# Three transposes of attention outputs moved from TensorE to DMA in a fused attention and mixture-of-experts kernel

## The chip, the cores and the metric

The kernel runs on one core of one Trainium2 chip. The core has a matrix engine (TensorE, PE in the profile), a vector engine (VectorE, DVE), an activation engine (ScalarE, ACT), a general engine (GpSimd, POOL) and a sequencer that mostly issues transfers (SyncE, SP). Each runs its own list of instructions in order, and waits on semaphores for the others. Sixteen DMA engines move data.

The metric is the device time of one execution in microseconds (us). The kernel before was run six times: the median is 678.63 us, the runs lie between 677.74 and 682.57.

## The reference

Two stages. First, attention over 4 batches, 8 heads, 768 positions and 64 dimensions a head. Each query sees its near keys (fewer than 16 positions away) and one summary key per block of 32 (the maximum of the block's keys, with the mean of its values):

```python
k_sum = k.reshape(B, H, nb, block, D).max(axis=3)
v_sum = v.reshape(B, H, nb, block, D).mean(axis=3)
scores_l_m = np.where(mask_l, scale * np.matmul(q, k.transpose(0, 1, 3, 2)), -1e9)
scores_s = scale * np.einsum('bhsd,bhnd->bhsn', q, k_sum) + np.log(block)
a = softmax(np.concatenate([scores_l_m, scores_s], axis=-1))
attn = np.matmul(a, np.concatenate([v, v_sum], axis=2))
```

Its output, as 3072 tokens of 512 features (`x`), goes to eight experts with a routing matrix that is normalised by rows and columns in turn, eight times:

```python
P = np.exp(x @ w_gate - max)
for _ in range(8):
    P /= P.sum(1, keepdims=True) + 1e-09
    P /= P.sum(0, keepdims=True) + 1e-09
    P *= N / E
for e in range(E):
    out += P[:, e:e + 1] * (np.maximum(x @ w1[e], 0.0) @ w2[e])
```

## The kernel before

**Tiling.** Attention is worked on in 16 pairs of heads; pair `i` belongs to batch `i // 4`, so pairs 12 to 15 are the last batch. Pairs 0 to 3 are done in halves, the others whole (`pair_whole`, line 687). A pair passes through these steps, named as the planner names them: the keys and queries are transposed (`tr`, line 295, tile tkq) and copied out (kT, qT); block sums of values (vs); block maxima of keys (km); scores (sg) and their exponential (er); the mask (em) and the edges of the window (Ee); scores of the block summaries (ss) and their exponential; `values` (line 389, tile av), the product with the values; `normalize` (line 487), which divides by the sums and writes the result as fp16 to the tile xs, 128 tokens by 6 x 128 features; `to_xT` (line 502), six 128x128 transposes on TensorE into a PSUM bank (tx); `x_out` (line 509), the copy from there to the persistent tile xT, on ScalarE or VectorE.

xs has two buffers for whole pairs, so `normalize` of pair i waits until the transposes of pair i-2 have read theirs (`U["xt", i - 2]`, line 712).

**Row copies.** `near_values` (line 346) copies edge rows of the values into the tile Ve by four small DMAs from SyncE. It waits until the values of pair i-2 have read that buffer. Until the output stores near the end of the program, SyncE issues nothing else.

**Fillers.** Attention alone does not fill TensorE, so the first expert (expert 0: `hidden_mm`, tile hps, and `project_mm`, tile yps, lines 198 to 211) is worked in between, for half batches whose xT is complete. When a batch's four pairs are through, `logits` (line 515, tile lp) computes its routing logits from xT, for all four pairs. After those of the last batch comes the routing normalisation (lines 1070 to 1101), beside the rest of expert 0 and the first groups of expert 1.

**The order.** It is made by a planner at build time (`Plan`, line 34). Each step is a unit with an engine, a planned cost in us, the units that it depends on, a priority, PSUM buffers that it opens or uses, and a lag, the time from its end until its result may be used. The planner simulates the engines with these figures and emits the units in the order in which they would start; the order in each engine's list is what it leaves behind. A cost that changes can move work on all engines. After attention the order is written out by hand (from line 1149): 6.08 us a group in the trace, experts 1 to 7 in a scheme that uses seven products in place of eight.

Of the kernel before, what the change touches and what calls it, by code (L numbers as in the profile page):

```python
# [33 lines left out]
class Plan:  # L34
# [12 lines left out]
    def add(self, eng, cost, fn, deps=(), prio=0.0, opens=(), uses=(), lag=0.0):  # L47
        u = Unit(eng, cost, fn, [d for d in deps if d is not None], prio, list(opens), lag)
        for b in list(opens) + list(uses):
            b.users.append(u)  # L50
        if uses and eng != "PE":
            u.prio -= 100.0
        self.waiting.append(u)
        return u
# [62 lines left out]
def kernel(  # L117
# [10 lines left out]
    nc = tc.nc  # L128

    B, H, S, D = q.shape  # L130
    G = S // 128
# [7 lines left out]
    PB = H // 2  # L139
# [20 lines left out]
    xT = persist.tile([128, KD, N], FP16)  # L160
# [34 lines left out]
    def copy(eng, out, in_):  # L195
        (nc.scalar.copy if eng == "ACT" else nc.vector.tensor_copy)(out=out, in_=in_)
# [19 lines left out]
    NE = 2  # L216
# [9 lines left out]
    if True:  # L226
# [16 lines left out]
        add = plan.add  # L243

        at, units = {}, {}

        def bank(tag, name, dtype=FP32):
            pool, n = (mps, 3) if tag == "m" else (aps, NA)
            return pool.tile([128, 2048 // mybir.dt.size(dtype)], dtype, tag=tag, name=name, bufs=n)
# [45 lines left out]
        def tr(i, z, tag):  # L295
            st = at.pop(("st", i, z))
            t = at["t", i, z] = bank(tag, "tkq", BF16)
            for g in range(G):
                if i < PB:
                    for j in range(2):  # L300
                        nc.tensor.transpose(t[64 * j:64 * j + 64, g * 128:(g + 1) * 128],
                                            st[:, j, g, :], ident)
                else:
                    nc.tensor.transpose(t[:, g * 128:(g + 1) * 128],  # L304
                                        st[:, g, :, :].rearrange("p j d -> p (j d)"), ident)

        def tr_out(eng, i, z):
            r, src = i % NB, at.pop(("t", i, z))[:, 0:S]
            dst = (kT[r][:], qT[r][:, W:W + S])[z]
            if i < PB:  # L310
                dst = dst.rearrange("c (p g) -> c p g", g=G)
                src = src.rearrange("c (g p) -> c p g", g=G)
            copy(eng, dst, src)
# [32 lines left out]
        def near_values(i):  # L346

            sv, ve = v_x[i % NQ], V_e[i % NE]
            for j in range(2):
                c0, q0 = VD * j, 64 + 32 * j  # L350
                nc.sync.dma_start(out=ve[q0 + W:q0 + 2 * W, 1:G, c0:c0 + VD],
                                  in_=sv[128 - W:128, j, 0:G - 1, :])
                nc.sync.dma_start(out=ve[q0:q0 + W, 0:G - 1, c0:c0 + VD],
                                  in_=sv[0:W, j, 1:G, :])

        def scores(i, h):
            sg = at["sg", i, h] = banks2("sg")
            for s in range(HG):
                for j in range(2):
                    score_mm(i, sg[:, j, s * LIVE:(s + 1) * LIVE], j, HG * h + s, 0, LIVE)  # L360

        def score_exp(i, h):
            if h == 0:
                at["er", i] = attn.tile([128, 2, G, LIVE], BF16, tag="er", name="er", bufs=2)
                at["em", i] = attn.tile([128, 2, G, 128], BF16, tag="em", name="em", bufs=2)
            nc.scalar.activation(
                out=at["er", i][:, :, HG * h:HG * (h + 1), :].rearrange("p j g l -> p j (g l)"),
                in_=at.pop(("sg", i, h))[:, :, 0:HG * LIVE], func=AF.Exp, bias=0.0, scale=SCALE)

        def masks(i, h):  # L370
            c = slice(HG * h, HG * (h + 1))
            nc.vector.tensor_tensor(
                out=at["em", i][:, :, c, :], in0=at["er", i][:, :, c, W:W + 128],
                in1=band[:, None, None, W:W + 128].to_broadcast([128, 2, HG, 128]), op=ALU.mult)

        def edges(i):
            ee, er = E_e[i % NE], at.pop(("er", i))
            for j in range(2):
                q0 = 64 + 32 * j
                nc.vector.tensor_tensor(out=ee[q0:q0 + 32, 0:G - 1, 128 - W:128],  # L380
                                        in0=er[0:32, j, 1:G, 0:W],
                                        in1=band[0:32, None, 0:W].to_broadcast([32, G - 1, W]),
                                        op=ALU.mult)
                nc.vector.tensor_tensor(out=ee[q0:q0 + 32, 1:G, 0:W],
                                        in0=er[96:128, j, 0:G - 1, W + 128:LIVE],
                                        in1=band[96:128, None, W + 128:LIVE].to_broadcast([32, G - 1, W]),
                                        op=ALU.mult)
# [114 lines left out]
        def to_xT(i, h=None):  # L502
            t = at.pop(("xs", i, h or 0))
            tx = at["tx", i, h] = bank("a", "tx", FP16)
            for g in range(G if h is None else HG):
                nc.tensor.transpose(tx[:, g * 128:(g + 1) * 128],  # L506
                                    t[:, g, :, :].rearrange("p j d -> p (j d)"), ident16)

        def x_out(eng, i, h=None):
            n, t0 = (S, 0) if h is None else (HS, h * HS)  # L510
            t0 += i // PB * S
            copy(eng, xT[:, i % PB, t0:t0 + n], at.pop(("tx", i, h))[:, 0:n])
# [92 lines left out]
        U = {}  # L605
# [79 lines left out]
            return U.get((what, n % PB, n // PB)) if n >= 0 else None  # L685

        def pair_whole(i, prio):
            U["near", i] = add("SP", 0.4, lambda: near_values(i), [U["v", i], U.get(("A", i - NE, 1))], prio,
                               lag=3.5)
            for h in range(2):  # L690
                buf = Buffer("s")
                U["S", i, h] = add("PE", 0.28, lambda h=h: scores(i, h),
                                   [U["kT", i, 0], U["kT", i, 1], U.get(("ed", i - 2))], prio, opens=[buf])
                U["X", i, h] = add("ACT", 0.97, lambda h=h: score_exp(i, h), [U["S", i, h]], prio, uses=[buf])
                U["mk", i, h] = add("DVE", 0.56, lambda h=h: masks(i, h),
                                    [U["X", i, h], U.get(("A", i - 2, 1))], prio)
            U["ed", i] = add("DVE", 0.78, lambda: edges(i),
                             [U["X", i, 0], U["X", i, 1], U["mk", i, 1], U.get(("A", i - NE, 1))], prio)
            bufs = [Buffer("a"), Buffer("a")]
            U["ss", i, 0] = U["ss", i, 1] = add("PE", 0.22, lambda: summaries2(i),  # L700
                                                [U["km", i], U["kT", i, 1], U.get(("A", i - NE, 1))], prio,
                                                opens=bufs)
            for h in range(2):
                U["sx", i, h] = add("ACT", 0.46, lambda h=h: summary_exp(i, h), [U["ss", i, h]], prio,
                                    uses=[bufs[h]])
            for h in range(2):
                buf = Buffer("a")
                U["A", i, h] = add("PE", 0.4, lambda h=h: values(i, h),
                                   [U["mk", i, h], U["ed", i], U["sx", i, h], U["Vs", i], U["near", i]],
                                   prio, opens=[buf])  # L710
                U["no", i, h] = add("DVE", 0.68, lambda h=h: normalize(i, h),
                                    [U["A", i, h], U.get(("xt", i - 2))], prio, uses=[buf])
            buf = Buffer("a")
            U["xt", i] = add("PE", 0.35, lambda: to_xT(i), [U["no", i, 0], U["no", i, 1]], prio, opens=[buf])
            U["x", i] = add({"ACT": 0.8, "DVE": 0.9}, 0, lambda: x_out(U["x", i].on, i), [U["xt", i]], prio,
                            uses=[buf])

        halves, zero = [], []

# [64 lines left out]
        for i in range(PB, NP):  # L784
# [3 lines left out]
            if i % PB == PB - 1:  # L788
                b = i // PB
                xs = [U["x", PB * b + d] for d in range(PB)]  # L790
# [24 lines left out]
    if True:  # L815
# [343 lines left out]
        g = q = NOTHING  # L1159
        for n in range(LAG, len(groups)):  # L1160
            g0, q0 = g, q
            g = group(*groups[n])
            q = pair(*groups[n - LAG])
            e, j, i = groups[n]
# [55 lines left out]
        A, B, C, D = last  # L1220
# [42 lines left out]
```

## Time and profile before

| what | value |
|---|---|
| median of six runs | 678.63 us |
| the profiled execution | 678.93 us |
| its span (first to last instruction) | 677.0 us |
| VectorE, ScalarE busy, share of the span | 86%, 60% |
| transposes tx<-xs, number, length of one | 96, 219 ns |
| xT<-tx copies of 128x768 on VectorE | 11, 558 ns each |
| DMA issue of a row copy on SyncE | 585 to 596 ns, at most 1405 |
| landing of a row copy, from its issue, whole span | 1.9 to 6.8 us, median 5.1 |

The difference between the execution's time and the span, 1.9 us, lies outside the instructions. An "idle before" in the profile names the engine and line whose end was last before the waiting instruction could start. Matmuls overlap their weight loads and each other, so the start-to-start distance of two groups is what a group takes from the queue, not the length shown. The first 100 us carry nearly all attention loads (DMA queues over 90% busy in the page's slices), and the stretch from 104 to 127 us, in which the last batch is finished, has quiet queues (3%).

### The profile page before, as it was taken

The page shows a single profiled execution, that of the slowest core. Times are in us where ns is not written, and L with a number is a line of the kernel's source. Part 1 is how long each engine was busy: PE and PEld are TensorE (multiplying, and loading weights), DVE is VectorE, ACT ScalarE, POOL GpSimd, SP SyncE. Part 2 cuts the span into 40 slices and gives each one's busy share as a digit, 9 for nine tenths or more (in the row PEclk, how much of TensorE's full clock was granted, in tenths as well). Part 3 has the DMA queues.
Part 4 walks back from the last instruction along what each step waited for, and adds up shares of the span by engine and source line. Part 5 has one row for each costly group of instructions (what it writes and reads, how often), then busy time and mean ns, then how long its engine had stood idle before and what let it go on. Part 6 is the DMA issues. An engine that isn't in the chain of part 4 may idle for free.

```text
span 677.0 us, 13655 instructions
## 1 busy us (share of the span) xinstructions
PE 666.7 (98%) x5189; PEld 438.8 (65%) x5189; DVE 582.9 (86%) x1440; ACT 406.3 (60%) x787; POOL 128.2 (19%) x171
## 2 busy tenths in 40 slices
PE   7999999999999999999999999999999999999996
PEld 4666666555666666666666666666666666666665
DVE  6878889688699988998889988998899888998885
ACT  4777787565677765555555655555555655556551
POOL 8599820112102010101011010101020101100001
PEclk9999999999999999999999999999999999999999
DMA  9999990000504041310513050405031141301224
GB/s 115 190 145 144 126 122 7 1 1 0 79 1 48 1 63 17 33 16 2 77 17 33 1 78 2 48 1 76 4 32 16 14 65 18 32 1 48 78 94 156
DMA packets 113618, 33.90 MB, mean 50 GB/s; under 512 B 99984, under 2 KB 110736, under 8 KB 113552
## 3 DMA queue, kind: packets, MB, share of 16 engines
q0 software_dynamic: 104672, 26.22, 41.4%
q1 hardware_dynamic: 8064, 6.27, 3.1%
q8 instruction: 40, 0.66, 0.4%
q10 hardware_dynamic: 816, 0.54, 0.2%
q14 instruction: 26, 0.21, 0.1%
HBM read 52.45 MB, written 6.29 MB: 87 GB/s over the span
## 4 chain that ended last, share of the span: by engine, by line
PE 93%; DVE 3%; DMA 1%; issue 1%; ACT 1%; POOL 0%; POOLq 0%; DVEq 0%; ACTq 0%
PE xy L889 36%; PE pg L883 16%; PE pa L883 11%; PE pb L883 11%; PE hps L200 6%; PE yps L210 6%; PE tkq L304 1%; PE sg L323 1%; DMA vx<-in_v_dram 1%; PE vs L331 1%; PE tx L506 1%; PE av L395 1%; PE av L401 1%; PE ss L419 1%; PE av L468 0%
## 5 line engine op out<-in xcount | busy, mean ns | idle before, releaser
L889 PEld LDWEIGHTS <-hf 128*128 128x128 f16 x2352 | 230.1, 98 | 96.0 <-issue 1.2
L889 PE MATMUL xy<-w,hf 128*128 128x256 f16 x1312 | 183.4, 273 | 0.1
L889 PE MATMUL xy<-ws,hf 128*128 128x256 f16 x984 | 147.6, 273 | 0.1
L191 ACT ACTIVATE hf<-pg 128x512 f16<-128x512 f32 x84 | 50.2, 597 | 150.3 <-PE pg L883 150.2
L1025 DVE SCALAR_TENSOR_TENSOR out_acc<-xy,P_sb,out_acc 128x512 f32<-128x512 f32 x164 | 115.0, 742 | 2.2 <-PE xy L889 2.2
L830 DVE TENSOR_TENSOR hf<-hf 128x512 f16<-128x512 f16 x252 | 99.1, 420 | 9.0 <-ACT hf L191 0.2
L883 PE MATMUL pa<-xT,w 128*128 128x512 f16 x336 | 99.9, 379 | 0.0
L883 PEld LDWEIGHTS <-w 128*128 128x128 f16 x672 | 65.8, 98 | 43.5
L833 DVE TENSOR_TENSOR hf<-pb,c 128x512 f16<-128x512 f32 x84 | 58.0, 691 | 37.1 <-PE pb L883 35.8
L176 POOL DMA_DIRECT2D w<-in_moe_w_dram x56 | 41.7, 756 | 220.3 <-PE pg L883 192.2
L883 PEld LDWEIGHTS <-ws 128*128 128x128 f16 x504 | 49.3, 98 | 25.3
L917 ACT COPY c<-pg 128x512 f32<-128x512 f32 x84 | 49.2, 586 | 22.7 <-PE pg L883 22.6
L833 DVE TENSOR_TENSOR hf<-pg,c 128x512 f16<-128x512 f32 x84 | 57.1, 680 | 0.2
L191 ACT ACTIVATE hf<-pa 128x512 f16<-128x512 f32 x84 | 50.6, 602 | 0.9 <-PE pa L883 0.9
L902 ACT COPY pg<-pa 128x512 f32<-128x512 f32 x84 | 47.9, 570 | 4.9
L883 PE MATMUL pb<-xTs,ws 128*128 128x512 f16 x168 | 50.0, 379 | 0.0
L883 PE MATMUL pb<-xT,ws 128*128 128x512 f16 x168 | 50.0, 379 | 0.0
L883 PE MATMUL pg<-xTs,ws 128*128 128x512 f16 x168 | 50.0, 379 | 0.0
L883 PE MATMUL pg<-xT,w 128*128 128x512 f16 x168 | 50.0, 379 | 0.0
L883 PE MATMUL pg<-xTs,w 128*128 128x512 f16 x168 | 50.0, 379 | 0.0
L910 ACT COPY c<-pb 128x512 f32<-128x512 f32 x84 | 49.7, 592 | 0.2 <-ACT pg L902 0.2
L200 PE MATMUL hps<-xT,w 128*128 128x384 f16 x256 | 49.4, 326 | 0.0
(137 smaller groups left out, 833.2 us busy)
## 6 DMA issues: line engine op xcount, KB each, us to landing
w<-in_moe_w_dram POOLq DMA_DIRECT2D x8, 1024.0 KB, 9.3
w<-in_moe_w_dram POOLq DMA_DIRECT2D x56, 128.0 KB, 3.5
out_dram<-out_acc SPq DMA_DIRECT2D x20, 256.0 KB, 2.0
qst<-in_q_dram POOLq DMA_DIRECT2D x32, 96.0 KB, 5.9
vx<-in_v_dram POOLq DMA_DIRECT2D x16, 192.0 KB, 6.6
kst<-in_k_dram POOLq DMA_DIRECT2D x24, 96.0 KB, 6.1
w<-in_moe_w_dram POOLq DMA_DIRECT2D x2, 512.0 KB, 8.5
kst<-in_k_dram POOLq DMA_DIRECT2D x4, 192.0 KB, 5.3
```

The source lines that it names most:

```text
L176: nc.gpsimd.dma_start(out=t[:, :, h, :], in_=moe_w1[e].rearrange("(dk p) f -> p dk f", p=128)[:, :, f:f + 128])
L191: nc.scalar.activation(out=out, in_=in_, func=AF.Relu, bias=0.0, scale=1.0)
L200: nc.tensor.matmul(hp[:, 0:n], lhsT=w1s[e][:, dk, 128 * f:128 * (f + 1)], rhs=xT[:, dk, t0:t0 + n], start=(dk == 0), stop=(dk == KD - 1))
L210: nc.tensor.matmul(yp[:], lhsT=h[:, f, c * 128:(c + 1) * 128], rhs=w2s[e][:, f, :], start=(f == 0), stop=(f == KF - 1))
L830: nc.vector.tensor_tensor(out=out, in0=in0, in1=in1, op=ALU.subtract)
L833: nc.vector.tensor_tensor(out=out, in0=in0, in1=in1, op=ALU.add)
L883: nc.tensor.matmul(bank[:], lhsT=w[:, dk, :], rhs=x[:, dk, :], start=start and dk == 0, stop=dk == KH - 1, skip_group_check=True)
L889: nc.tensor.matmul(bank, lhsT=a(f)[:, 128 * c:128 * (c + 1)], rhs=w[:, f, :], start=start and f == 0, stop=f == FH - 1, skip_group_check=True)
L902: nc.scalar.copy(out=B["g"][:], in_=B["a"][:])
L910: nc.scalar.copy(out=B["c5"][:], in_=B["b"][:])
L917: nc.scalar.copy(out=B["c2"][:], in_=B["g"][:])
L1025: nc.vector.scalar_tensor_tensor(out=acc, in0=src, scalar=P_sb[:, t, e:e + 1], in1=acc, op0=ALU.mult, op1=ALU.add)
```

## The change

For pairs 12, 13 and 14, the six transposes on TensorE and the copy out of PSUM are replaced by one transposing DMA from SyncE, which reads xs in SBUF and writes xT in SBUF. Pair 15 keeps the old way. In the planner it is one unit of 1.25 us on SyncE with a lag of 4.5, which stands both for "xs has been read" and for "xT is there". The unit of the row copies is planned with 2.5 us on SyncE and a lag of 1.9, in place of 0.4 and 3.5; its instructions are the same.

```diff
+        def x_dma(i):
+            nc.sync.dma_start_transpose(
+                out=xT[:, i % PB, i // PB * S:(i // PB + 1) * S].rearrange("c (g t) -> c g t", g=G),
+                in_=at.pop(("xs", i, 0))[:].rearrange("p g j d -> p (g j d)"))
+
...
         def pair_whole(i, prio):
-            U["near", i] = add("SP", 0.4, lambda: near_values(i), [U["v", i], U.get(("A", i - NE, 1))], prio,
-                               lag=3.5)
+            U["near", i] = add("SP", 2.5, lambda: near_values(i), [U["v", i], U.get(("A", i - NE, 1))], prio,
+                               lag=1.9)
...
-            buf = Buffer("a")
-            U["xt", i] = add("PE", 0.35, lambda: to_xT(i), [U["no", i, 0], U["no", i, 1]], prio, opens=[buf])
-            U["x", i] = add({"ACT": 0.8, "DVE": 0.9}, 0, lambda: x_out(U["x", i].on, i), [U["xt", i]], prio,
-                            uses=[buf])
+            if 12 <= i < 15:
+                U["xt", i] = U["x", i] = add("SP", 1.25, lambda: x_dma(i), [U["no", i, 0], U["no", i, 1]], prio,
+                                             lag=4.5)
+            else:
+                buf = Buffer("a")
+                U["xt", i] = add("PE", 0.35, lambda: to_xT(i), [U["no", i, 0], U["no", i, 1]], prio, opens=[buf])
+                U["x", i] = add({"ACT": 0.8, "DVE": 0.9}, 0, lambda: x_out(U["x", i].on, i), [U["xt", i]], prio,
+                                uses=[buf])
```

## The prediction

> **What bounds the kernel now.** I read the page first: engine totals, then the chain of work that ended last.
>
> ```profile
> span 677.0 us, 13655 instructions
> ...
> PE 666.7 (98%) x5189; PEld 438.8 (65%) x5189; DVE 582.9 (86%) x1440; ACT 406.3 (60%) x787; POOL 128.2 (19%) x171
> ...
> PE 93%; DVE 3%; DMA 1%; issue 1%; ACT 1%; POOL 0%; POOLq 0%; DVEq 0%; ACTq 0%
> ```
>
> TensorE is busy 98% of the span and carries 93% of the chain. But matmuls overlap, so "busy" is not enough: what counts is whether each group starts as soon as the one before lets it. So I went to TensorE's timeline between 103 and 127 us, where batch 3 is worked on and where the change acts. Columns: start, length, engine, line, what, how many.
>
> ```profile
> 104.11 0.50 PE L506 MATMUL tx<-ident,xs 128*128 128x128 f16 x6
> 104.45 1.03 PE L210 MATMUL yps<-w,h 128*128 128x512 f16 x4
> ...
> 110.12 0.50 PE L506 MATMUL tx<-ident,xs 128*128 128x128 f16 x6
> 110.45 1.03 PE L210 MATMUL yps<-w,h 128*128 128x512 f16 x4
> ...
> 117.05 0.50 PE L506 MATMUL tx<-ident,xs 128*128 128x128 f16 x6
> 117.38 0.81 PE L200 MATMUL hps<-xT,w 128*128 128x384 f16 x4
> ...
> 126.59 0.74 PE L520 MATMUL lp<-wg_bf,xT 128*128 128x8 f16 x24
> ```
>
> These are the transposes of pairs 12, 13 and 14, what follows each, and the logits of batch 3. Each group begins before the one ahead has ended by its modelled length, and no wait is shown. So the stage is a dense queue: what is taken out moves all behind it. After the logits the order of TensorE is the same in both programs, and the timeline from 172 us on is a steady 6.08 us per group (xy at 176.06, 182.14, 188.22) with TensorE at the end of the waits. Later work follows the logits one for one, the routing normalisation included, since it starts from them.
>
> **What is removed.** Three groups of six transposes. By starts: 104.45-104.11 = 0.34, 110.45-110.12 = 0.33, 117.38-117.05 = 0.33, together **1.00 us** of TensorE. The "0.50" is a pipelined length, not what the queue pays. With them go three copies xT<-tx on VectorE (0.56 us each, 1.7 in all). VectorE is not on the path here, so they count nothing by themselves.
>
> [...] In this trace six cost 0.33 us, 56 ns each. [...]
>
> **What moves.** The planner lays out the order anew. No engine's order differs before the place of pair 12's transposes, so the new cost of the row copies (0.4 to 2.5 us of SyncE, lag 3.5 to 1.9) changes nothing in batches 1 and 2: cost 0. POOL's order is unchanged. From 104.1 us TensorE has the same work minus 18 transposes, with fillers (hps, yps) set elsewhere. A switch to 64-row work costs a little (yps x4 takes 0.87 us before a full-height group, 0.95 from 104.45 to 105.40); the new order has about as many such switches, so I put 0, within 0.1 either way. Shared terms cancel, and the logits can start at 126.59-1.0, about 125.6, if no new wait bites. I laid the new order out by hand with the start-to-start steps of this trace to find the places. Main ones: values of pair 13 at 107.0 (was 107.3), of pair 14 at 113.0 (113.96), scores of pair 15 at 114.0 (112.99, later, as the plan put them behind pair 14's values), its summaries at 119.05 (118.12), its values at 121.1 (122.09), its transposes, still on TensorE, at 123.5 (124.53).
>
> **What is added: three transposing DMAs on SyncE, and their waits.** SyncE's row in the trace, tile Ve between 100 and 112 us (counts, then min/median/max in ns, first and last start):
>
> ```profile
> L351 SPq DMA_DIRECT2D Ve<-vx x4: 586/590/594, 102.4 to 109.5; - x4
> L353 SPq DMA_DIRECT2D Ve<-vx x4: 595/596/1172, 103.0 to 110.1; - x4
> ...
> DMA to landing us min/median/max: 1.9/1.9/3.2
> ```
>
> These are the row copies of pairs 14 (102.4 to 105.5) and 15 (108.2 to 110.7); the DMA queues are otherwise quiet (3% busy from 104 to 127). SyncE's new order is: four copies of 14, transpose 12, four copies of 15, transposes 13 and 14, then output stores, hundreds of us later. Each transpose moves 128x768 x 2 bytes = 192 KB.
>
> Issue time: not in the trace. Lower end one copy's 0.59 us; upper end six blocks at 0.59, 3.5 us. Copies of pair 15 queue behind transpose 12, which starts at 105.5. They wait for the values of pair 13 (about 107.8), so 2.3 us of issue is hidden. At 3.5 they start at 109 and land by 114.7, while the values of pair 15 need them at 121. Cost 0 at both ends.
>
> Landing time T, from issue: not in the trace. Lower end: the row's 1.9 us plus the bytes. [...] I take **6 us**, the middle, near the 5.75 that the new code books (1.25 + 4.5); neither end can be negative.
>
> Who waits. (a) xs has two buffers, so the normalisation of pair 14 waits for transpose 12 to land. VectorE gets there at about 113.4, issue was at 105.5: it is hidden up to T = 7.9. Behind that instruction stand, on VectorE, a relu, the w2 differences, the block maximum and masks of pair 15; the summaries of pair 15 want that maximum with some 0.65 us to spare. (b) Pair 15's normalisation waits for transpose 13: issue 110.2, wanted 121.6, hidden up to 11.4. (c) The logits wait for transpose 14: its issue follows pair 14's normalisation, ending at about 114.9 (the present row, copied below, takes 1.8 us for the two halves with a filler in between), wanted 125.6: hidden up to 10.7.
>
> ```profile
> 114.64 0.18 DVE L498 RECIPROCAL rc<-av 128x6 f32<-128x6 f32 x1
> 114.86 0.56 DVE L499 TENSOR_TENSOR xs<-av,rc 128x384 f16<-128x384 f32 x1
> 115.33 0.41 DVE L205 TENSOR_TENSOR w<-w 128x512 f16<-128x512 f16 x1
> 115.66 0.19 DVE L498 RECIPROCAL rc<-av 128x6 f32<-128x6 f32 x1
> 115.89 0.56 DVE L499 TENSOR_TENSOR xs<-av,rc 128x384 f16<-128x384 f32 x1
> ...
> 125.06 0.56 DVE L196 COPY xT<-tx 128x768 f16<-128x768 f16 x1 [0.94 <-PE tx L506]
> ```
>
> At 6 us all three are hidden. Then what is late next is pair 15's own chain: its xT copy ends at 125.6 now and about 124.6 then, a microsecond before the logits, as before.
>
> **Sum.** -1.0 (transposes), 0 (VectorE's copies, switches, SyncE's issues and waits) = **-1.0 us**. The profiled execution took 678.93 us (span 677.0 and 1.9 around it), so 677.9. The median of the six is 678.63, 0.3 lower: **677.6 us**. That is 0.15%, within the 0.3% (2.0 us) that a measurement of this kernel can tell from no change.
>
> **Rivals.**
> - *Slow transposes (slower).* Place: waits (a) and (c), which add up, since pair 14's normalisation starts no sooner than 105.5+T, takes 1.45, and its own transpose needs T again: logits at 107.0+2T. That passes the new 125.6 from T = 9.3, the old 126.59 from T = 9.8, and 2.0 us more from T = 10.8. TensorE runs in order, with no filler behind the logits that doesn't need this xT. At T = 12 they start at 131.0, 4.4 us late: 683.0. [...] Against it: quiet queues, and 3.2 us is the worst landing in this stretch.
> - *The gain is eaten (same).* Pair 15's chain has less cover: its key copy on ScalarE moves from 110.46 to about 111.6, its scores are 1.0 later, its summaries and edges have 0.65 to 0.75 us to spare where 0.8 to 1.3 stood. Were these rows half a microsecond to 1.5 longer, or T 8 to 9.5, between half and all of the gain would go: 678.0 to 678.7. Against it: the rows repeat within 2%.
> - *The change reaches further (faster).* The row copies' new cost could re-order batches 1 and 2. It doesn't: the orders are equal there. What batch 3 can give is bounded by the 1.0 and a tenth of switches, so more than 2.0 could only be spread of the runs (677.74 to 682.57 before).
>
> **How the numbers follow.** Forecast 0.63: 677.2 to 678.0 and the runs' spread. Gain eaten 0.15: 678.0 to 679. Slow transposes 0.17: 680.7 and up. The rest 0.05, below 676.6. So faster by over 0.3% 0.05, within 0.3% 0.78, slower 0.17. The range goes from 676.8 (full gain, half a microsecond of spread) up into the slow case to T = 10.8, 680.6; above lies some 0.15, below 0.05.
>
> **What would show it.** Right: TensorE's groups stay touching between 104 and 127 us, tx shows 78 transposes for 96, logits start near 125.6, transposes 12 to 14 land within 8 us, and no VectorE wait names them. Wrong: VectorE idle ahead of pair 14's xs, or TensorE idle ahead of lp, released by a DMA into xT; SyncE's transposes taking over 3.5 us to issue; or touching groups and logits at 126.6, where the layout lost what the transposes gave.

## The result, and the profile after

The changed kernel took 677.07 us in the median of 36 runs (676.28 to 681.32), the kernel before, run beside it, 679.15 in 73 (677.43 to 683.47). The ratio is 0.9966 with a 95% interval of 0.9956 to 0.9976. It is a ratio of means, 677.44 and 679.75: 2.3 us faster, where 1.0 was forecast. In part of the executions of either kernel TensorE's mean granted clock is lower (under 0.998: down to 0.994 after, and to 0.990 in the runs of the kernel before beside the experiments) and the time some microseconds longer; without those above 679 us (38 of 73 before, 5 of 36 after) the medians are 678.29 and 676.90, 1.39 us apart, and this second difference is the better one to hold against a sum of instructions.

The page of the changed kernel (span, busy times, chain of waits):

```profile
span 675.3 us, 13625 instructions
...
PE 666.4 (99%) x5171; PEld 437.8 (65%) x5171; DVE 582.4 (86%) x1439; ACT 405.3 (60%) x785; POOL 128.2 (19%) x171
...
PE 94%; DVE 2%; POOL 1%; DMA 1%; issue 1%; ACT 0%; POOLq 0%; DVEq 0%; ACTq 0%
```

TensorE has 18 instructions fewer (5189 before) and is as much the bound as ever. Its timeline in the stage of the change, in the same columns as before:

```profile
101.92 0.51 PE L304 MATMUL tkq<-ident,kst 128*128 128x128 bf16 x6
...
103.13 0.50 PE L304 MATMUL tkq<-ident,qst 128*128 128x128 bf16 x6
103.56 0.53 PE L336 MATMUL vs<-vx,m_blk 128*64 128x128 bf16 x6
...
122.98 0.50 PE L511 MATMUL tx<-ident,xs 128*128 128x128 f16 x6
123.32 1.89 PE L210 MATMUL yps<-w,h 128*128 128x512 f16 x8
125.05 0.74 PE L525 MATMUL lp<-wg_bf,xT 128*128 128x8 f16 x24
...
170.61 0.60 PE L898 MATMUL xy<-w,hf 128*128 128x256 f16 x4
```

Behind the query transposes of pair 14 (103.13) come block sums, where before the six tx of pair 12 stood; the only tx left is pair 15's. No line here carries a wait. Two lines of the kernel before are needed beside them:

```profile
102.57 0.51 PE L304 MATMUL tkq<-ident,kst 128*128 128x128 bf16 x6
...
172.16 0.60 PE L889 MATMUL xy<-w,hf 128*128 128x256 f16 x4
```

The logits start 1.54 us earlier than before (126.59), but 0.65 of that was there already at the query transposes of pair 14 (103.78 before), ahead of anything that the change re-orders. A clock that starts at the key transposes of pair 14, the first line, is better: from there to the logits it is 23.13 us, against 102.57 to 126.59, 24.02, before. **The stage gained 0.89 us.** To the first product of the hand-written part (xy, 170.61 and 172.16) it is 68.69 against 69.59, so 0.90 arrives there undiminished.

The transposing DMAs, the rows of their source line (counts, then min/median/max in ns, first and last start in us):

```profile
L308 SPq DMA_TRANSPOSE xT<-xs x3: 1212/1237/1587, 105.5 to 114.5; - x3
...
who waited for it (us, times):
...
DMA to landing us min/median/max: 2.7/2.8/3.1
```

Issuing one takes SyncE 1.2 to 1.6 us, landing 2.7 to 3.1 from the start of its issue, and the list of who waited is empty. TensorE's logits at 125.05 carry no wait, and VectorE's timeline confirms it at the two other places where one could have come, the normalisations of pairs 14 and 15:

```profile
113.23 0.56 DVE L504 TENSOR_TENSOR xs<-av,rc 128x384 f16<-128x384 f32 x1
...
121.10 0.20 DVE L503 RECIPROCAL rc<-av 128x6 f32<-128x6 f32 x1 [1.53 <-PE av L406]
```

Pair 14 writes its buffer at 113.23, five microseconds after pair 12's transpose, issued at 105.5, has landed. Pair 15 waits for TensorE's products, not for a transfer.

### The profile page after: what moved, and what is told of

The parts are those of the page before. It is cut to its first block, busy times and chain, and to the rows that moved or that the text cites. A ratio compares the mean times of both kernels' runs of the same rounds, so it can differ in the third digit from the quotient of the medians.

```text
span 675.3 us, 13625 instructions
## 1 busy us (share of the span) xinstructions
PE 666.4 (99%) x5171; PEld 437.8 (65%) x5171; DVE 582.4 (86%) x1439; ACT 405.3 (60%) x785; POOL 128.2 (19%) x171
## 4 chain that ended last, share of the span: by engine, by line
PE 94%; DVE 2%; POOL 1%; DMA 1%; issue 1%; ACT 0%; POOLq 0%; DVEq 0%; ACTq 0%
PE xy L898 37%; PE pg L892 16%; PE pa L892 11%; PE pb L892 11%; PE hps L200 6%; PE yps L210 6%; PE sg L328 1%; PE tkq L304 1%; DMA qst<-in_q_dram 1%; PE vs L336 1%; PE av L473 1%; PE av L400 1%; PE tx L511 1%; PE av L406 1%; PE ss L424 1%
```

## The experiments

Three theories were tested first. **Q**: the gain is TensorE's queue time, about 0.33 us a pair, and the rest of the difference is spread. **W**: the DMA brings more than that, 2.3 us. **N**: the new planning figures of the row copies bring part of it. "Stage" below is the time from the key transposes of pair 14 to the logits of the last batch; "to xy" goes on to the first xy. Ratios are of means, each to the runs of the kernel before that stood beside the same kernel. Stage and way to xy repeat within 0.02 us from kernel to kernel where nothing was changed, while the times of runs scatter by a microsecond and more.

| kernel | runs | median us | ratio to before | stage us | to xy us |
|---|---|---|---|---|---|
| before (profile) | 73 | 679.15 | 1 | 24.02 | 69.59 |
| after (profile) | 36 | 677.07 | 0.9966 [0.9956, 0.9976] | 23.13 | 68.69 |
| near_only | 12 | 678.84 | 0.9991 [0.9970, 1.0011] | 24.02 | 69.59 |
| dma_only | 12 | 676.85 | 0.9965 [0.9946, 0.9984] | 23.13 | 68.70 |
| extra18 | 12 | 678.62 | 0.9995 [0.9975, 1.0015] | 24.13 | 69.70 |
| twice | 12 | 677.54 | 0.9990 [0.9972, 1.0007] | 23.13 | 68.70 |
| thrice | 6 | 685.83 | 1.0103 [1.0079, 1.0127] | 29.33 | 76.25 |
| before_warm | 12 | 679.29 | 1.0000 [0.9986, 1.0013] | 24.02 | 69.59 |
| after_warm | 12 | 677.34 | 0.9969 [0.9955, 0.9984] | 23.13 | 68.69 |
| tiny18 | 12 | 677.66 | 0.9982 [0.9964, 1.0000] | 23.13 | 69.15 |

near_only, dma_only, extra18 and pairs8_14 ran on one chip, twice, thrice, pairs8_14_lag and pairs4_14 on a second, and the last three of the table on a third; each chip has its own runs of the kernel before. The kernels of more pairs have another order, and so no stage to compare; they follow below.

### near_only and dma_only: one part of the change at a time

near_only is the kernel before with the new figures of the row copies alone:

```diff
-            U["near", i] = add("SP", 0.4, lambda: near_values(i), [U["v", i], U.get(("A", i - NE, 1))], prio,
-                               lag=3.5)
+            U["near", i] = add("SP", 2.5, lambda: near_values(i), [U["v", i], U.get(("A", i - NE, 1))], prio,
+                               lag=1.9)
```

> Only the planner's figures for the row copies change (2.5 and lag 1.9 for 0.4 and 3.5); the transposes stay on TensorE. Every engine's list has the order of the kernel before. Theory Q (the gain is TensorE's queue, 0.33 us for each pair's six transposes, 1.0 us in all; what the comparison of the result shows above that is the spread of executions): ratio 1.000 within its interval. Theory N (the new figures for the row copies bring part of the 2.3 us): about 0.998. Theory W (the DMA brings more than the queue time, 2.3 us for three pairs): 1.000. Whatever it shows away from 1.000 is what two runs of one order differ by.

dma_only is the changed kernel with this edit taken back.

> The DMA transposes of pairs 12 to 14 with the old planner figures for the row copies; the order on every engine is that of the changed kernel. Q: ratio 0.9985 (1.0 us). N: nearer to 1 than the changed kernel's 0.9966. W: 0.9966. Both Q and W: same profile as the changed kernel, transposes issued in 1.2 to 1.6 us and landed 2.7 to 3.1 us after issue.

near_only's stage, by TensorE's timeline:

```profile
102.06 0.51 PE L304 MATMUL tkq<-ident,kst 128*128 128x128 bf16 x6
...
126.08 0.74 PE L520 MATMUL lp<-wg_bf,xT 128*128 128x8 f16 x24
```

126.08 - 102.06 = 24.02, as before; dma_only has 23.13, as after. The planning figures are worth nothing in the stage (and the ratio of near_only, 0.9991, has 1 in its interval), so N falls, and the DMA is the whole change. Between Q and W the two readings of dma_only disagree: its stage gains what Q expects, but its ratio, 0.9965, is W's 0.9966, and Q's 0.9985 lies just outside the interval.

### extra18: the queue time given back

The changed kernel, with the transposes of pair 14's keys and queries and of pair 15's keys done twice: 18 transposes of 128x128 more, in the stage from which 18 were taken.

```diff
-            for g in range(G):
+            for g in [*range(G)] * (2 if (i, z) in ((14, 0), (14, 1), (15, 0)) else 1):
```

> The changed kernel with 18 transposes of the same shape put back on TensorE, in the same stretch: the input transposes of pair 14 (keys and queries) and of pair 15 (keys) are done twice, with the same result. Nothing else moves. Q: back to the kernel before, ratio 1.000, and the logits of batch 3 1.0 us later, relative to the stretch before, than in the changed kernel. W: still about 1.3 us faster, 0.998.

```profile
102.13 0.84 PE L304 MATMUL tkq<-ident,kst 128*128 128x128 bf16 x12
103.68 0.83 PE L304 MATMUL tkq<-ident,qst 128*128 128x128 bf16 x12
111.03 0.83 PE L304 MATMUL tkq<-ident,kst 128*128 128x128 bf16 x12
...
126.26 0.74 PE L525 MATMUL lp<-wg_bf,xT 128*128 128x8 f16 x24
```

The stage is 24.13: exactly 1.00 more than with the DMA alone, the price that was taken from start-to-start distances. The ratio, 0.9995, is back at the kernel before, as Q expected, though its interval holds W's 0.998 too; so it is the stage that decides. What the change gains there is TensorE's time: where that is given back, nothing is left. The stage had gained 0.89 rather than 1.00: extra18, with as many transposes as the kernel before, takes 0.11 more, which is what the new order costs.

### twice and thrice: how late may the transpose be?

Each transposing DMA is issued two or three times into the same place; each waits for the one ahead (2.7 to 4.3 us from issue to landing in twice, 2.7 to 3.1 in thrice), and SyncE is held meanwhile. The edit of twice (thrice has 3):

```diff
+            t = at.pop(("xs", i, 0))
+            for _ in range(2):
                 nc.sync.dma_start_transpose(
...
```

> The changed kernel with each of the three transposing DMAs issued twice into the same place; the second waits for the first, so one transpose takes about twice the 2.8 us from issue to landing, 5.6, and SyncE is held for the time between. Theory of the hidden landing: pair 12's transpose lands at about 111 us, before pair 14's normalisation wants the buffer at 113.0; pair 14's lands at about 121.5, before the logits at 125: no TensorE and no VectorE wait, ratio to before as with one DMA (0.9965), about 676.9 us. Rival, that landing time is paid in part on the path: the logits are 2.8 us later, about 679.6 us, ratio about 1.001.

> The same with three in a row, 8.4 us from the first issue to the last landing. SyncE is in order: pair 12's ends its issue at about 112.3, pair 15's row copies come behind it, pair 13's first starts at about 114.7 and its last lands at 123, pair 14's first starts at about 121.5 and its last lands at about 130. Theory of the hidden landing, with SyncE's order: TensorE idle for about 4.5 to 5 us ahead of the logits, released by a DMA into xT; span about 680, time about 681.5 us, ratio about 1.003. By the prediction's formula for slow transposes, 107.0 + 2T with T = 8.4 and no queue on SyncE, the logits would start at 123.8, that is, nothing is lost: 676.9 us.

With two, the stage is 23.13 and TensorE has no wait in it: 5.6 to 7.1 us from first issue to last landing cost nothing. The ratio of 0.9990 came out above the 0.9965 expected, though the profiled stage is the same to the hundredth; 3 of its 12 executions had a mean clock under 0.998. The medians of the others, 677.46 against 678.58 for the kernel before, are 1.1 us apart, near to the stage's 0.9. With three, 8.4 to 8.6 us, TensorE's timeline shows this:

```profile
129.79 0.34 PE L513 MATMUL tx<-ident,xs 128*128 128x128 f16 x3 [2.08 <-DVE xs L506]
130.48 0.34 PE L513 MATMUL tx<-ident,xs 128*128 128x128 f16 x3 [0.35 <-DVE xs L506]
130.66 1.89 PE L210 MATMUL yps<-w,h 128*128 128x512 f16 x8
132.39 0.20 PE L527 MATMUL lp<-wg_bf,xT 128*128 128x8 f16 x2
135.71 0.75 PE L527 MATMUL lp<-wg_bf,xT 128*128 128x8 f16 x22 [3.12 <-DMA xT<-xs]
136.32 1.44 PE L200 MATMUL hps<-xT,w 128*128 128x384 f16 x4
```

Two of the 24 logits matmuls still go at 132.39; the stage is counted to 135.71, where the rest follow. VectorE's timeline, at the normalisations of pairs 14 and 15:

```profile
118.46 0.56 DVE L506 TENSOR_TENSOR xs<-av,rc 128x384 f16<-128x384 f32 x1 [0.81 <-DMA xT<-xs]
...
129.17 0.56 DVE L506 TENSOR_TENSOR xs<-av,rc 128x384 f16<-128x384 f32 x1 [3.31 <-DMA xT<-xs]
```

The first is wait (a). VectorE stood ready 7.9 us after pair 12's issue at 109.7, as the prediction had said; TensorE did not wait for it. What cost time is that three in a row held SyncE from 109.7 to 116.8, 7.1 us (two landings of 2.7 to 3.1 and an issue of 1.2), twice the upper end of 3.5 that the prediction had for issue. Pair 15's row copies came behind, and pair 13's transpose began at 120.4 only. So pair 15's normalisation stood 3.31 us for its buffer (wait (b), which the prediction had thought the safest), TensorE then 2.08 and 0.35, and the logits, for pair 14's transpose, 3.12. That is 5.55 us of TensorE, and the stage is 6.20 longer, where 4.5 to 5 was expected from SyncE's queue; the time is 685.83, where 681.5 was expected. The prediction's formula, 107.0 + 2T, would have let 8.4 us pass for nothing; but it speaks of one transfer that lands late and leaves SyncE free, and such a one was not run in this stage. The last line of TensorE's timeline tells of a second cost: four hps take 1.44 us, not 0.81. The windows of the same kernel (first the window's length, then busy us and instructions of PE, PEld, DVE, ACT and POOL; the last three are granted clock, DMA share, GB/s):

```profile
134.00:138.00 4.00, 2.29 (x28) 1.35 (x29) 1.19 (x4) 0.42 (x2) 0.42 (x1) 0.71 0.25 49
138.00:142.00 4.00, 4.00 (x23) 2.29 (x22) 3.48 (x13) 2.00 (x5) 0.10 (x1) 0.87 0.02 4
```

The clock fell behind the wait of 3.12, and to xy the loss has grown from 6.20 to 7.55 us. So this wait of TensorE cost more than its length. The wait of 2.08 did not do this: the eight yps behind it take 1.73 us from start to start, as in twice, and the granted clock from 128 to 134 us was 1.00. The slack that the change lives on is real, but bounded: for transposes that hold SyncE as these do, it runs out between 7.1 and 8.4 us.

### pairs8_14, pairs8_14_lag and pairs4_14: would more pairs give more?

If each pair is worth 0.3 us, one would move more of them.

```diff
-            if 12 <= i < 15:
+            if 8 <= i < 15:
```

> DMA transposes for pairs 8 to 14, seven in place of three. Q: 7 x 0.33 = 2.3 us, ratio 0.9966, if all seven land within what the waits allow (about 8 us from issue; 2.7 to 3.1 seen in the changed kernel, more where weight and input loads fill the queues, before some 100 us). W: seven thirds of 2.3 us, 5.4 us, ratio 0.992. A wait that bites: nearer to 1, with VectorE idle ahead of xs, released by DMA, in the timeline.

It came out at 677.05 in the median of 12 runs (0.9973 [0.9948, 0.9997]), where dma_only, beside it, has 676.85 and 0.9965: no gain clear of the noise. (Of its 12 executions 5 had a mean clock under 0.998; the median of the others is 676.46.) From the key transposes at 60 us to xy it takes 110.43 us, where near_only takes 111.19 and dma_only 110.30: four pairs more lose 0.13 where 1.33 was to be gained. To the logits it is 64.19 against 64.73, with one hps group more on the way (4 matmuls, 0.65 us start to start); so 1.19 of the 1.33 was still there, and was lost behind them. TensorE's timeline behind the logits says where the gain went:

```profile
126.14 0.81 PE L200 MATMUL hps<-xT,w 128*128 128x384 f16 x4
127.73 0.36 PE L1095 MATMUL sink<-csum_sb,col_en 128*128 128x8 f32 x2 [0.78 <-DVE csum_sb L1090]
```

The planner, with work gone from batch 2, had put one hps group ahead of the logits that in the changed kernel stands behind them, and 4 instead of 16 hps ahead of the first column total. That is too little to cover the column sums on VectorE: 0.78 us of TensorE are lost there, of the 1.32 that go between the logits and xy. The transposes themselves landed in 2.7 to 11.7 us, and VectorE stood 0.8 us once for its buffer, but TensorE did not wait for them. The next kernel has the same work on TensorE, with 2.8 in place of 2.0 us planned for that wait:

```diff
-                    step = add(eng, us, fn, [step], -50.0, opens=o, uses=w, lag=(1.2 if n else 2.0) if fn is columns else 0.0)
+                    step = add(eng, us, fn, [step], -50.0, opens=o, uses=w, lag=(1.2 if n else 2.8) if fn is columns else 0.0)
```

> DMA transposes for pairs 8 to 14, and in the planner a lag of 2.8 in place of 2.0 us behind the first column sums of the routing, which puts two more groups of hps ahead of the first column total; every instruction is the same as in pairs8_14. Theory (TensorE's queue, with the extra 1.33 us of pairs 8 to 11 lost in the routing, where TensorE sat idle 0.78 us for the column sums, and in what followed): the idle time goes, 0.8 to 1.4 us less than pairs8_14, 675.1 to 675.7 us at full clock, ratio 0.995 to 0.996. Rival (batch 2's transposes lose their gain in batch 2 itself, by landings of up to 11.7 us among the loads): no faster than pairs8_14, 676.5 us, ratio 0.997.

```profile
128.69 0.28 PE L1095 MATMUL sink<-csum_sb,col_en 128*128 128x8 f32 x2
...
135.16 0.39 PE L1095 MATMUL sink<-csum_sb,col_en 128*128 128x8 f32 x2 [0.34 <-DVE csum_sb L1090]
136.36 0.59 PE L892 MATMUL pg<-xT,w 128*128 128x512 f16 x2 [0.81 <-DVE xT L839]
```

The first wait is gone, and 0.34 and 0.81 us stand seven microseconds later, again for VectorE. From 60 us to xy: 110.39. The measured 677.50 (12 runs, 0.9984 [0.9973, 0.9995]) is no gain either. Both theories of this expectation failed: the gain was not lost in batch 2, and the wait that was found was not all that stood between it and the end. In the routing of both kernels it is VectorE that TensorE waits for.

pairs4_14 moves eight pairs more, into the stretch in which the loads still run.

> DMA transposes for pairs 4 to 14, eight pairs more than the change. Theory of TensorE's queue alone: 8 x 0.333 = 2.7 us less than the changed kernel, about 674.2 us at full clock, ratio about 0.993. Rival, contention with the loads: until about 92 us the DMA queues are about 90% busy, landings there were up to 11.7 us in pairs8_14, so pairs 4 to 7 make VectorE's normalisation wait for its buffer and hold up TensorE; half of the gain or more is given back, 676 us or later, ratio 0.996 or above.

```profile
76.17 0.53 PE L336 MATMUL vs<-vx,m_blk 128*64 128x128 bf16 x6 [1.34 <-DVE xs L504]
...
80.95 0.48 PE L200 MATMUL hps<-xT,w 128*128 128x384 f16 x1 [2.10 <-DMA xT<-xs]
81.22 0.82 PE L525 MATMUL lp<-wg_bf,xT 128*128 128x8 f16 x24
81.90 1.44 PE L200 MATMUL hps<-xT,w 128*128 128x384 f16 x4
```

685.38 us in 6 runs, ratio 1.0096 [1.0082, 1.0110]: the contention rival was right, but put the loss far too low. The same transfer that lands in 2.8 us in the changed kernel took 6.1 to 10.6 between 40 and 100 us (median 8.2), and now TensorE waits: 0.83 and 0.32 us for ScalarE, 1.34 and 0.41 for VectorE's xs, and 2.10 for a transpose, between 72 and 81 us, 5.0 in all. The hps behind it run at 1.44 for 0.81 again; the granted clock was 0.92 from 60 to 85 us and 0.95 from 85 to 110, by estimate 0.50 from 81 to 87.

### before_warm and after_warm: the executions with the low clock

In the profiles of thrice and pairs4_14 the clock was low at the start too, long before their transposes. This is thrice's start, TensorE's timeline and then the windows, in their columns:

```profile
13.59 0.80 PE L338 MATMUL vs<-vx,m_blk 128*64 128x128 bf16 x6 [2.04 <-DMA vx<-in_v_dram]
```

```profile
12.00:14.00 2.00, 0.41 (x5) 0.41 (x5) 0.34 (x1) 0.28 (x1) 1.86 (x3) 0.69 1.83 145
14.00:16.00 2.00, 2.00 (x18) 1.03 (x18) 1.17 (x4) 0.77 (x2) 1.91 (x3) 0.50 1.62 166
16.00:20.00 4.00, 4.00 (x52) 2.77 (x48) 2.25 (x5) 1.99 (x3) 2.97 (x5) 0.50 1.58 189
```

TensorE had waited 2.04 us there for the values of pair 1 to land (1.77 in pairs4_14). So four matmuls on zeros were put ahead of that step, in the kernel before and in the changed one:

```diff
+            t = bank("a", "vs")
+            for _ in range(4 if i == 1 else 0):
+                nc.tensor.matmul(t[:], lhsT=zeros[:], rhs=zeros[:, None, :].to_broadcast([128, 4, 128]), start=True, stop=True)
-            vs = at["vs", i] = bank("a", "vs")[0:64, 0:2 * D]
+            vs = at["vs", i] = t[0:64, 0:2 * D]
```

> The kernel before with four matmuls on zeros (0.21 us each, 0.86 in all) ahead of the block sums of pair 1, at about 12 us, where TensorE waits for the values of pair 1 to land. In the profiles of two kernels that wait was 1.8 and 2.0 us, and the granted clock was 0.50 from 14 to 20 us; in all others it was 1.24 us at most and the clock 1.00. Theory S (the executions at 679 to 684 us are those in which this start-up wait is long, and have nothing to do with the change): executions with a mean clock under 0.998 become rare (14 of 35 before on the first chip), the fastest ones lose 0 to 0.6 us, median 678.3 to 678.9. Rival (another cause of the lower clock): as many such executions as in the kernel before.

> The changed kernel with the same four matmuls ahead of the block sums of pair 1. Theory S with theory Q (the change gives TensorE's queue of about 1 us and little else): its median is 0.9 to 1.4 us under that of the kernel before with the same four matmuls, 677.0 to 677.6, and the lower clocks are rare in both. Rival W (the change brings 2.3 us by itself): 2.0 us or more under it.

All 24 executions had a mean clock of 0.998 or more; beside them 9 of 29 of the kernel before did not. Theory S holds: with TensorE busy in the wait at 12 us those executions are gone. The two kernels differ by 1.95 us in their medians, between the 0.9 to 1.4 of theory Q and the 2.0 or more of W, nearer to W, so neither was met. Their way to xy differs by 0.90 (69.59 and 68.69). The other 1.05 has no place in the two profiles: ahead of the stage, where the two have the same work, the profiled execution of after_warm, its slowest, is the later one (103.60 against 102.48). By the medians the four matmuls, 0.86 us long, cost the kernel before 0.94 (679.29 against 678.35, that of its runs beside it with a mean clock of 0.998 or more), where 0 to 0.6 was expected, and the changed one about 0.4 (677.34 against 676.90, which comes from other chips). Why they cost less there isn't shown.

As a version, after_warm is no step forward: its worst run is 678.69, not 681.32, but its mean of 677.43 us is that of the changed kernel (677.44).

### tiny18: is it the number of instructions?

Outside the span lay 1.66 to 1.76 us in every execution of the changed kernel, but up to 2.8 in the kernel before, and also in extra18. These two share 5189 TensorE instructions, where the changed kernel has 5171; the 18 more are transposes in both. To tell the number from the transposes, the changed kernel got 18 small matmuls:

```diff
+            if b == B - 1:
+                for n in range(18):
+                    t, dk = b * G + n // 3, n % 3
+                    nc.tensor.matmul(lp[:, n // 3 * E:(n // 3 + 1) * E], lhsT=xT[:, dk, t * 128:(t + 1) * 128],
+                                     rhs=wg_bf[:, dk, :], start=(dk == 0), stop=(dk == 2))
```

> The changed kernel with 18 of the last batch's 24 logits matmuls (128x8) issued twice, so that TensorE has as many instructions as before (5189), but only 18 x 25 ns = 0.45 us more to do. The time outside the span was 1.7 to 1.8 us in every execution with 5171 or fewer, and 1.7 to 2.8 in those with 5189. If the number of instructions decides this, the time outside spreads again, mean about 2.0; if it is the transposes themselves or something else of theirs, it stays at 1.7 to 1.8. Theory Q: logits group 1.06 us long in place of 0.60, time 677.3 at full clock, ratio 0.997 to 0.998.

The way to xy grew by 0.46 us, as 18 x 25 ns wants. Of its 12 executions 4 had more than 1.85 us outside the span (up to 2.18, mean 1.80). So it needs no transposes; but before_warm, with 5193, had none above 1.83. The spread was seen with 5189 TensorE instructions in four kernels (before, near_only, extra18, tiny18), and with no other count (5123, 5147, 5171, 5175, 5193). Why, stays open.

## Why the prediction was right or wrong

- *TensorE's dense queue is the bound, and later work follows the logits one for one.* Right: stage and way to xy gained 0.89 and 0.90, and extra18 loses 1.00 for 18 transposes.
- *1.00 us for the three groups, by start-to-start.* Right, by extra18 to the hundredth. In the queue the 18 cost 56 ns each.
- *Switches and fillers: 0, within 0.1 either way.* 0.11, a loss (extra18 against the kernel before).
- *Row copies' figures: 0.* Right (near_only).
- *Issue time, 0.59 to 3.5 us, cost 0.* 1.21 to 1.59, cost 0.
- *Landing time T = 6.* 2.8 from issue to landing (2.7 to 3.1). No run shows the 6: it was the author's estimate, near the 5.75 that the new code books. The mechanism and the cost (nothing) were right, the size was off by half; twice shows that 5.6 would have been free too. The lower end was the near one: 2.8 is 0.9 above the row copies' 1.9 us, from which it started.
- *Wait (a) hidden to 7.9, (b) to 11.4, (c) to 10.7, each by its own T.* Never reached in the changed kernel. Thrice shows that the places were right, and (a) to the tenth; (b) and (c) bit at 8.4, as three in a row hold SyncE longer than any issue time that the prediction had followed through the queue.
- *Sum -1.0, so 677.6, and more than 2.0 could only be spread of the runs.* What it summed was mis-sized by 0.1, and the other half of the sentence holds in part. That the measured 677.07 lies near the forecast is in part luck: the difference, 2.1 by medians and 2.3 by means, is twice the sum, and the base of six runs, 678.63, lay 0.5 under the median of 73. (The range has a slip: 677.6 less half a microsecond is 677.1, not 676.8; the measured median falls on that edge.) Of the 2.3, some 0.9 goes with the longer executions, 38 of 73 against 5 of 36. This is a cut by time; of the 87 runs of the kernel before beside the experiments 35 lay above 679, and 29 of these had a mean clock under 0.998. Of the 1.39 that is left, the stage is 0.9 and the time outside the span some 0.2 (means of 1.83 to 2.00 in three sets of the kernel before, 1.70 in the changed one). The rest is not located. At a mean clock of 0.998 or more the median span of dma_only is 1.3 us under that of the kernel before on its chip (675.1 and 676.4), that of twice 0.9 (675.7 and 676.6), where the stage gives 0.89 in both; so 0 to 0.4. It may lie ahead of the stage: there the work is the same, and yet the profiles at full clock and without the four matmuls on zeros reach the stage anywhere between 101.82 us (tiny18) and 102.57 (the kernel before).
- *The spread itself.* The weakest step is that the prediction took it for symmetric noise: the six runs, 677.74 to 682.57, already showed a tail, and a mean over 73 holds it while one profile does not. By before_warm and after_warm the low clock hangs on the wait at 12 us, which the change does not touch by its order. Whether its lower share in kernels with the DMA is caused or chance isn't settled: on one chip the kernel before had 14 of 35, near_only 4 of 12, dma_only 1 of 12, but pairs8_14 5 of 12.
- *Rivals.* Slow transposes: the place was right, but the landing was never near (thrice made a like case). Gain eaten: not in the changed kernel, but with four pairs more, in part by VectorE in the routing and not by pair 15's chain. The change reaches further: the measured ratio is on that side, just past 0.3%, and got a chance of 0.05 only; by near_only the planner's figures, that rival's first reason, were not the cause, and its second, the spread of the runs, was in part.

## What to carry to other kernels

Price what leaves a dense TensorE queue by start-to-start distances, then check it by putting the same number back elsewhere: an interval between two fixed marks in the profile repeats to 0.02 us where times of runs scatter by 1. Moving a transpose to DMA paid here as long as other work covered its landing (2.8 us with quiet queues, 6.1 to 10.6 among the loads), so choose quiet queues and count what stands behind it on the issuing engine; four more pairs brought nothing that could be told from noise, as the stage that followed then waited for another engine, and eight more, reaching into the loads, were a loss. Look at the spread of the runs before forecasting: a tail has a place in the program, too.

## What the hardware showed that was not expected

- A transposing DMA of 192 KB from SBUF to SBUF: 1.21 to 1.59 us of issue for SyncE, 2.7 to 3.1 from issue to landing with quiet queues (the changed kernel, DMA share 0.16 from 104 to 127 us), 6.1 to 10.6 among the loads (pairs4_14).
- A wait of TensorE was paid more than once: in thrice 6.20 us to the logits had grown to 7.55 at xy. At 12 us, waits of up to 1.50 us left the clock at 1.00 in the profiles, and 1.77 and 2.04 us (pairs4_14, thrice) were followed by 0.50 from 14 to 20 us, and by 0.66 and 0.62 from 20 to 24. In mid-program 2.10 us (pairs4_14) and 3.12 (thrice) were followed by four hps in 1.44 us, not 0.81, and by a lower clock (0.92 from 60 to 85 us, 0.71 from 134 to 138), but 2.08 (thrice) was not (1.00 from 128 to 134), so the length of one wait doesn't decide it alone.
- The time outside the span scatters (1.66 to 2.83 us) in the four kernels with 5189 TensorE instructions and does not (1.66 to 1.83) in the others, for a reason that these runs do not show.
